# Spectral mixing plus MLP on one core: VectorE and ScalarE work of block 1 behind additions and copies

## The chip, the cores and the metric

The kernel runs on one core of a Trainium2 chip. The metric is the device time of one execution in microseconds, as the median of several runs. The core's engines work side by side, each through its own instructions in a fixed order: TensorE (PE in the profile) multiplies matrices, VectorE (DVE) and ScalarE (ACT) work element by element, GpSimd (POOL) starts some transfers and reduces over partitions, and SyncE (SP) issues most transfers. They wait for each other by semaphores.

## The reference

Tokens `x` (2048 x 576) are normalized; the result is the sum of `x`, a two-dimensional Fourier mixing of the normalized tokens (real part), and a ReLU MLP of them with 4608 hidden units.

```python
def _A_ref(x, dft_seq_re, dft_seq_im, dft_hid_re, dft_hid_im):
    a = jnp.einsum("bsd,ed->bse", x, dft_hid_re)
    b = jnp.einsum("bsd,ed->bse", x, dft_hid_im)
    return jnp.einsum("ts,bse->bte", dft_seq_re, a) - jnp.einsum("ts,bse->bte", dft_seq_im, b)

def _B_ref(x, w1, w2):
    h = jnp.maximum(jnp.einsum("bsd,df->bsf", x, w1), 0)
    return jnp.einsum("bsf,fd->bsd", h, w2)

xn = _layernorm(x, axis=-1)
return x + _A_ref(xn, A_dft_seq_re, ...) + _B_ref(xn, B_w1, B_w2)
```

## The kernel before, in words

Every operand of float32 is split into two float16 halves, a high one (a ScalarE copy) and a low one (a VectorE subtraction), and a product is three float16 matmuls. The weights are scaled by powers of two before they are split: VectorE takes the maximum of their magnitudes (`max_w1`, the reductions at L117 and L625), GpSimd reduces it over the partitions (`power`, L123), VectorE works out the scale from that (L126 to L131: `half`, `c_sw`, `c_pw`), and then `split` (L185 on ScalarE, L186 on VectorE) writes the halves.

The MLP is done in 9 blocks `b` of 512 hidden units by 4 groups `g` of 512 tokens: 36 steps `n`, numbered `b * 4 + g`. One step does the first layer of (b, g) (`mlp1_step`, L346 and L371; four accumulators `p1_b_g_0` to `_3` in PSUM) and, between its parts, the second layer of the step before (`mlp2`, L589), whose seven products 0 to 6 are those of a scheme that needs seven products instead of eight for a 2 x 2 blocked multiplication. This is why sums of blocks are needed: sums of w2's blocks (`sums_w2`, L712 to L715), sums of h's blocks, and, from block 2 on, where the first layer is done by the same scheme, sums of w1's blocks and of the tokens' blocks.

`mlp1_out` takes the hidden values out of PSUM, one pair of accumulators at a time (pair 0 and pair 1 of each step): ReLU to the high halves on ScalarE (L390, L394), the low halves on VectorE (L395), four sums of blocks on VectorE (L399 to L402), their high halves on ScalarE (L404) and their low halves on VectorE (L406). Product 1 of `mlp2` reads what L394 and L395 wrote, products 2 to 5 read the sums.

`mlp2` accumulates products in PSUM places: 0, 2, 4 and 6 in one, 1 in another, 3 and 5 in a third, with two buffers for them all. Behind each product its place is read: by a ScalarE copy (L600) behind products 0, 2, 3 and 6, by a VectorE addition (L603) behind 1, 4 and 5. A product in the same place waits for that reader. So product 6 waits for the addition behind product 4, product 4 for the copy behind product 2, product 5 for the copy behind product 3. GpSimd then adds the sums to HBM (L606, `spill`).

`sums_x` is a generator of 10 pieces a group. Each group needs four sums of token blocks, on VectorE (L469 to L473), with high halves on ScalarE (L453) and low halves on VectorE (L458). Block 2 reads them first. In block 1 `next(tq)` takes a piece behind each product of `mlp2`, and some more at the end of a quarter of the step.

`todo` is a list of the preparations of the next block's weights, in order: loads of w1, its maxima and scale, its splits, loads of w2, their maxima and scale, splits, sums, splits. `work()` takes one piece from it. The raw weights come into two buffers (`raw`), so w2's loads (L100, issued by SP) wait until w1's splits have read theirs. In step 2 (block 0, group 2) block 1's list begins:

```python
if n == 2:
    if i > 1:
        todo += prepare_block(1) if i == 2 else []
        for _ in range(1 if i == 2 else 11):
            work()
    continue
```

A scheduler takes the traced instructions and lays down each engine's order when the kernel is built. `tc.issue_after(ins)` puts the instructions of its block behind `ins` on the same engine, without a semaphore. `behind(key)` does it for the last instruction that was noted under a name: `"vfree"` is VectorE's last addition of a product, `"free"` ScalarE's last copy of one.

Of the kernel before, what the change touches and what calls it, by code (L numbers as in the profile page):

```python
# [13 lines left out]
AF = mybir.ActivationFunctionType  # L14
ALU = mybir.AluOpType
# [34 lines left out]
def kernel(  # L50
# [17 lines left out]
    nc = tc.nc  # L68
# [123 lines left out]
    means, factors, shifts, order = {}, {}, {}, {}  # L192
# [4 lines left out]
    def behind(key):  # L197

        return tc.issue_after(order[key]) if key in order else nullcontext()
# [118 lines left out]
    A11, A12, A22, S1, S2, S3, S4 = range(7)  # L318
# [57 lines left out]
            ps.append(new_ps1(b, g, 0))  # L376
        mlp1_group(b, g, i, slice(0, G), ps[i], WK[:-1], start=(i == 0), stop=(i > 0))

    def mlp1_out(b, g, i, pa, pb, after=None, last=None):

        h = hs[b, g, i] = mlp.tile([P, 2, 7, GH], F16, tag="h", name=f"h{b}_{g}_{i}", bufs=4)
        st = mlp.tile([P, 5, GH], F32, tag="stage", name=f"s{b}_{g}_{i}")
        stt = nc.vector.scalar_tensor_tensor
        a11, a21, a12, a22 = pa[:, :GH], pa[:, GH:], pb[:, :GH], pb[:, GH:]
        r21, s1, s2, s3, s4 = (st[:, n] for n in range(5))
        with behind(after):
            nc.scalar.activation(r21, a21, AF.Relu)  # L390
        for q, src in ((slice(A11, A11 + 1), a11), (slice(A12, A22 + 1), pb)):
            hi, lo = (h[:, n, q].rearrange("p a b -> p (a b)") for n in range(2))
            with behind(after):
                order["hi"] = nc.scalar.activation(hi, src, AF.Relu).ins  # L394
                stt(lo, src, 0.0, hi, ALU.max, ALU.subtract)  # L395

        def sums():
            with behind(last or after):
                stt(s3, a11, 0.0, r21, ALU.max, ALU.subtract)  # L399
                stt(s1, a22, 0.0, r21, ALU.max, ALU.add)  # L400
                stt(s2, a22, 0.0, s3, ALU.max, ALU.subtract)
                stt(s4, a12, 0.0, s2, ALU.max, ALU.subtract)  # L402
            hi, lo = (h[:, n, S1 : S4 + 1] for n in range(2))
            order["s"] = nc.scalar.activation(hi, st[:, 1:], AF.Copy).ins  # L404
            with behind(last):
                order["lo"] = nc.vector.tensor_tensor(lo, st[:, 1:], hi, ALU.subtract).ins  # L406

        if last:
            return sums
        sums()  # L410

# [14 lines left out]
    def halves(g, q):  # L428

        r, c = q  # L430
        k, t = 2 * r, (H1, H2)[c]
        return xT[g][:, k : k + 2, t], xT[g][:, KM + 1 + k : KM + 3 + k, t]
# [7 lines left out]
    def sums_x(g):  # L440

        f = [
            w[:, 2 * KT * P :][:, : 2 * GH].rearrange("p (k t) -> p k t", t=GH) for w in w1bufs[2:]
        ]
        tt = nc.vector.tensor_tensor

        def high(q):
            with tc.issue_after(gates[g][0]):
                nc.scalar.activation(xsums[g][:, q, 0], f[q % 2], AF.Copy)  # L453

        def low(q):
            hi, lo = (xsums[g][:, q, n] for n in range(2))
            with tc.issue_after(gates[g][1]):
                tt(lo, f[q % 2], hi, ALU.subtract)  # L458

        for q, (head, tail) in enumerate((  # L460
            ((0, 1), (0, 0)), ((1, 1), None), ((1, 0), None), ((1, 1), (0, 1)),
        )):
            if q > 1:
                low(q - 2)
            t = f[q % 2]
            h, l = halves(g, head)
            if tail:
                h2, l2 = halves(g, tail)
                tt(t, h, h2, ALU.subtract)  # L469
                tt(t, t, l2, ALU.subtract)  # L470
            else:
                tt(t, h, f[1 - q % 2], ALU.subtract)
            tt(t, t, l, ALU.add)  # L473
            yield
            if q:
                high(q - 1)
            yield
        low(2)
        high(3)
        yield  # L480
        low(3)
        yield

    banks1, ends, gates = [], [], {}
# [534 lines left out]
    for n in range(2, len(steps)):  # L1019
# [46 lines left out]
        ps = []  # L1066
        for i in range(NF):
# [12 lines left out]
                transposes_dma(t, nc.scalar)  # L1080
            if i % 2:
                after = ("w2hi", "vfree")[i // 2] if n == 2 else None
                mlp1_out(b, g, i // 2, *ps[i - 1 : i + 1], after=after)
            if i == (3 if n == 2 else 1):

                gates[n - 2] = order["s"], order["lo"]
            if n == 2:
                if i > 1:
                    todo += prepare_block(1) if i == 2 else []
                    for _ in range(1 if i == 2 else 11):  # L1090
                        work()
                continue
            if b:
                work()
            for q in range(2 * i, min(2 * i + 2, 7)):
                mlp2(pb, pg, q)
                if b:
                    next(tq, None)
                else:
                    for _ in range(2):  # L1100
                        work()
            for _ in range((0, 1, 0, 2)[i] if b else 0):
                next(tq, None)
            for _ in range(1 + i % 2 if b else (2, 2, 2, 4)[i]):
                work()
            if (n, i) > (6, 1) and i % 2 and passes:
# [1 line left out]
        if n == 2:  # L1108
            for q in range(2, 7):
                mlp2(pb, pg, q)  # L1110
    while todo:
        work()
    for q in range(7):
# [239 lines left out]
```

## Time and profile before

| what | value |
|---|---|
| median of 3 runs | 1249.34 us (1249.05 to 1249.57) |
| the profiled execution | 1249.3 us |
| its span in the trace | 1247.5 us |
| mean granted TensorE clock | 0.999 |
| first products of block 2 (L512) in the trace | 200.87 us |

The times of the trace are counted from the span's start. A row of a timeline has the start and the duration in us, the engine, the line, the operation, what it writes and reads, the shape and a count; in brackets stands how long the engine was idle before it, and who released it. The duration of one row runs on into the next by some 0.08 us, so a step is best read from start to start. A row of the waits has the total in us, how often, and the longest. A row of the windows has, for a stretch, the busy time of each engine with its number of instructions, and at its end the granted clock of TensorE (1.00 is full), the share of time in which the transfer engines worked, and GB/s.

### The profile page before, as it was taken

What the parts mean: (1) busy time and instruction counts of PE and PEld (TensorE: products, weight loads), DVE (VectorE), ACT (ScalarE), POOL (GpSimd) and SP (SyncE); (2) the same over time, 40 slices, a digit from 0 to 9 for tenths busy, and PEclk for the clock granted to TensorE, in tenths of its full rate; (3) what the DMA queues carried; (4) which work ended last, traced back from release to release, by engine and by line L of the source; (5) the groups of instructions that cost most, each with busy time, mean ns of one, the idle gap of its engine ahead of it and who ended that gap; (6) DMA issues with size and microseconds to landing.
All of it is one profiled execution on the core that took longest, in us unless ns stands there. A gap on an engine that the chain in (4) does not pass through costs nothing.

```text
span 1247.5 us, 25273 instructions
## 1 busy us (share of the span) xinstructions
PE 1228.4 (98%) x10269; PEld 981.0 (79%) x10269; DVE 1009.1 (81%) x1919; ACT 704.7 (56%) x1192; POOL 158.9 (13%) x207
## 2 busy tenths in 40 slices
PE   8989999999999999999999999999999999999998
PEld 7656557888888888888888888877777777777776
DVE  9999997878878788788787878467787878888885
ACT  5655465676676765766777766545543333333332
POOL 2321221212121211111111112200000000000000
PEclk9999999999999999999999999999999999999999
DMA  9985356757667665666585766620053434443420
GB/s 313 204 134 125 59 85 140 130 126 145 144 103 174 120 150 117 134 139 134 119 176 120 160 128 124 130 83 1 1 173 124 133 117 148 134 127 125 136 87 20
DMA packets 80324, 157.28 MB, mean 126 GB/s; under 512 B 22224, under 2 KB 41168, under 8 KB 80208
## 3 DMA queue, kind: packets, MB, share of 16 engines
q1 hardware_dynamic: 57424, 113.20, 28.6%
q0 software_dynamic: 22784, 42.48, 25.9%
q8 instruction: 80, 1.31, 0.5%
q14 instruction: 36, 0.29, 0.1%
HBM read 104.53 MB, written 51.90 MB: 125 GB/s over the span
## 4 chain that ended last, share of the span: by engine, by line
PE 83%; DVE 7%; ACT 1%; issue 1%; DMA 1%; POOL 0%; POOLq 0%; DVEq 0%; ACTq 0%
PE p L1285 26%; PE p L589 24%; PE bank L512 23%; PE pd L1156 8%; DMA raw_w<-in_w_dram 1%; PE p L346 1%; DVE w2s L186 1%; DVE h L395 1%; DVE dbuf L473 1%; DVE acc L458 0%; DVE c_mf L117 0%; PE pd L1166 0%; DVE w1buf L186 0%; ACT f L1008 0%; DVE dbuf L470 0%
## 5 line engine op out<-in xcount | busy, mean ns | idle before, releaser
L589 PE MATMUL p<-w2s,h 128*128 128x288 f16 x3024 | 410.2, 287 | 9.2 <-DVE c_sw L127 4.1
L589 PEld LDWEIGHTS <-h 128*128 128x128 f16 x3024 | 296.1, 98 | 86.0 <-issue 10.6
L1285 PE MATMUL p<-R,cs 128*128 128x288 f16 x2688 | 329.4, 286 | 0.0
L1285 PEld LDWEIGHTS <-cs 128*128 128x128 f16 x2688 | 263.0, 98 | 66.3
L185 ACT ACTIVATE cs<-c,sc_c 128x1024 f16<-128x1024 f32 x112 | 125.2, 1144 | 196.7 <-DVE c L1218 72.6
L186 DVE SCALAR_TENSOR_TENSOR cs<-c,sc_c,cs 128x1024 f16<-128x1024 f32 x112 | 141.0, 1282 | 54.4 <-ACT cs L185 54.4
L512 PEld LDWEIGHTS <-w1buf 128*128 128x128 f16 x1600 | 156.5, 98 | 21.6 <-issue 0.5
L512 PEld LDWEIGHTS <-dbuf 128*128 128x128 f16 x1200 | 117.4, 98 | 15.8
L512 PE MATMUL bank<-xT,w1buf 128*128 128x256 f16 x832 | 109.8, 273 | 0.0
L1156 PE MATMUL pd<-dbuf,xT 128*128 128x288 f16 x832 | 103.8, 286 | 0.0
L512 PE MATMUL bank<-acc,w1buf 128*128 128x256 f16 x768 | 102.3, 273 | 0.3 <-ACT acc L538 0.3
L534 DVE TENSOR_TENSOR h<-s,h 128x1024 f16<-128x1024 f32 x56 | 68.5, 1224 | 37.9 <-ACT h L531 37.9
L1156 PEld LDWEIGHTS <-xT 128*128 128x128 f16 x832 | 80.8, 98 | 22.0 <-issue 1.9
L606 POOL DMA_DIRECT2D spill<-dbuf x70 | 61.0, 874 | 241.7 <-DVE dbuf L603 214.6
L519 ACT ACTIVATE h<-acc 128x256 f16<-128x256 f32 x112 | 46.0, 411 | 71.5 <-DVE acc L542 70.6
L512 PE MATMUL bank<-xT,dbuf 128*128 128x256 f16 x624 | 82.3, 273 | 0.0
L531 ACT ACTIVATE h<-s 128x1024 f16<-128x1024 f32 x56 | 59.2, 1056 | 35.4 <-DVE s L526 35.1
L512 PE MATMUL bank<-acc,dbuf 128*128 128x256 f16 x576 | 76.6, 273 | 0.0
L1291 DVE SCALAR_TENSOR_TENSOR o<-p,us_c,o 128x288 f32<-128x288 f32 x112 | 57.5, 514 | 12.9 <-PE p L1285 12.5
L600 ACT ACTIVATE dbuf<-p,c_ub 128x576 f32<-128x576 f32 x70 | 51.3, 733 | 22.3 <-PE p L589 22.0
L1008 ACT ACTIVATE f<-f 128x1024 f32<-128x1024 f32 x60 | 62.7, 1046 | 0.4 <-DMA f<-in_cre_dram 0.4
L520 DVE SCALAR_TENSOR_TENSOR h<-acc,h 128x256 f16<-128x256 f32 x112 | 47.3, 422 | 18.7 <-ACT h L519 18.3
(163 smaller groups left out, 1519.8 us busy)
## 6 DMA issues: line engine op xcount, KB each, us to landing
spill<-dbuf POOLq DMA_DIRECT2D x70, 288.0 KB, 5.2
c<-in_cre_dram SPq DMA_DIRECT2D x32, 512.0 KB, 4.3
c<-in_cim_dram SPq DMA_DIRECT2D x32, 512.0 KB, 5.0
f<-in_cre_dram SPq DMA_DIRECT2D x30, 512.0 KB, 5.9
f<-in_cim_dram SPq DMA_DIRECT2D x30, 512.0 KB, 5.8
spill<-sum POOLq DMA_DIRECT2D x42, 288.0 KB, 4.5
raw_w<-in_w_dram SPq DMA_DIRECT2D x17, 640.0 KB, 5.6
raw_w<-in_w_dram SPq DMA_DIRECT2D x18, 576.0 KB, 5.0
```

The lines of the kernel that those rows point to most:

```text
L185: nc.scalar.activation(hi, src, AF.Copy, scale=s).ins,
L186: nc.vector.scalar_tensor_tensor(lo, src, s, hi, ALU.mult, ALU.subtract).ins,
L512: nc.tensor.matmul(ps, l, r, start=first and m == 0, stop=m == len(todo) - 1, skip_group_check=not first,)
L531: order["s"] = nc.scalar.activation(hi_s, st[:, 1:], AF.Copy).ins
L534: order["lo"] = nc.vector.tensor_tensor(lo_s, st[:, 1:], hi_s, ALU.subtract).ins
L589: order["pe"] = nc.tensor.matmul(ps[:, c], h[:, x, qa, c * P : (c + 1) * P], w[:, y, qb], start=first and i == 0 and j == 0, stop=i == NQ ...
L600: freed(nc.scalar.activation(o, ps, AF.Copy, scale=us[b]))
L606: nc.gpsimd.dma_start(spill[g, row, col], o, accum_op=ALU.add)
L1008: nc.scalar.activation(f, f, AF.Abs, scale=2.0**-10, accum_out=sums_c[:, n, q : q + 1])
L1156: nc.tensor.matmul(ps[j], xT[g][:, kx, c * P : (c + 1) * P], dsp[j][:, hl, k], start=(t % 2 == 0 and n == 0), stop=(t % 2 == 1 and n == le ...
L1285: nc.tensor.matmul(ps, w[:, a, k], r[:, c, rq], start=first and k == 0 and j == 0, stop=k == HK - 1 and j == 2, skip_group_check=not first,)
L1291: order["o"] = nc.vector.scalar_tensor_tensor(o, ps, us["c"][:, n : n + 1], o, ALU.mult, ALU.add).ins
```

## The change

Four things are moved; no operation is added or removed.

1. In step 2, 4 pieces of block 1's list are taken at the place where 11 were, and the other 7 behind the last products of `mlp2` of that step. The reductions of the second half of w1 and all of w1's splits therefore stand behind the additions of group 1, and the splits behind those of group 2's first products as the scheduler lays them.
2. For pair 0 in block 1, the high halves of the sums (ScalarE) are emitted behind product 3 and put behind its copy, and the low halves (VectorE) behind product 5 and its addition.
3. The pieces of `sums_x` are taken in three bunches a step, behind products 0, 2 and 3, and 6, instead of one behind each product and some between.
4. For groups 1 to 3 the sums of tokens and their low halves are put behind the last addition of a product.

```diff
-    def mlp1_out(b, g, i, pa, pb, after=None, last=None):
+    def mlp1_out(b, g, i, pa, pb, after=None, last=None, late=False):
...
-        def sums():
+        def values():
             with behind(last or after):
                 stt(s3, a11, 0.0, r21, ALU.max, ALU.subtract)
                 stt(s1, a22, 0.0, r21, ALU.max, ALU.add)
                 stt(s2, a22, 0.0, s3, ALU.max, ALU.subtract)
                 stt(s4, a12, 0.0, s2, ALU.max, ALU.subtract)
-            hi, lo = (h[:, n, S1 : S4 + 1] for n in range(2))
-            order["s"] = nc.scalar.activation(hi, st[:, 1:], AF.Copy).ins
-            with behind(last):
+
+        hi, lo = (h[:, n, S1 : S4 + 1] for n in range(2))
+
+        def high():
+            with behind("free" if late else None):
+                order["s"] = nc.scalar.activation(hi, st[:, 1:], AF.Copy).ins
+
+        def low():
+            with behind("vfree" if late else last):
                 order["lo"] = nc.vector.tensor_tensor(lo, st[:, 1:], hi, ALU.subtract).ins
 
         if last:
-            return sums
-        sums()
+            return lambda: (values(), high(), low())
+        values()
+        if late:
+            return high, low
+        high()
+        low()
...
         def low(q):
             hi, lo = (xsums[g][:, q, n] for n in range(2))
-            with tc.issue_after(gates[g][1]):
+            with tc.issue_after(gates[g][1]), behind("vfree" if g else None):
                 tt(lo, f[q % 2], hi, ALU.subtract)
...
-            if tail:
-                h2, l2 = halves(g, tail)
-                tt(t, h, h2, ALU.subtract)
-                tt(t, t, l2, ALU.subtract)
-            else:
-                tt(t, h, f[1 - q % 2], ALU.subtract)
-            tt(t, t, l, ALU.add)
+            with behind("vfree" if g else None):
+                if tail:
+                    h2, l2 = halves(g, tail)
+                    tt(t, h, h2, ALU.subtract)
+                    tt(t, t, l2, ALU.subtract)
+                else:
+                    tt(t, h, f[1 - q % 2], ALU.subtract)
+                tt(t, t, l, ALU.add)
...
-                mlp1_out(b, g, i // 2, *ps[i - 1 : i + 1], after=after)
+                late = mlp1_out(
+                    b, g, i // 2, *ps[i - 1 : i + 1], after=after, late=bool(b) and i == 1
+                )
...
-                    for _ in range(1 if i == 2 else 11):
+                    for _ in range(1 if i == 2 else 4):
                         work()
...
             for q in range(2 * i, min(2 * i + 2, 7)):
                 mlp2(pb, pg, q)
                 if b:
-                    next(tq, None)
+                    if q in (3, 5):
+                        late[q == 5]()
+                    for _ in range((2, 0, 3, 2, 0, 0, 3)[q]):
+                        next(tq, None)
                 else:
                     for _ in range(2):
                         work()
-            for _ in range((0, 1, 0, 2)[i] if b else 0):
-                next(tq, None)
...
         if n == 2:
             for q in range(2, 7):
                 mlp2(pb, pg, q)
+            for _ in range(7):
+                work()
```

## The prediction

> **What bounds the kernel now.** I read the page first, then the waits of TensorE in stretches, then the windows and the timelines of the engines around each wait, and at last the order in which the changed kernel is built, engine by engine.
>
> ```profile
> span 1247.5 us, 25273 instructions
> ...
> PE 1228.4 (98%) x10269; PEld 981.0 (79%) x10269; DVE 1009.1 (81%) x1919; ACT 704.7 (56%) x1192; POOL 158.9 (13%) x207
> ```
>
> TensorE (PE) is busy in 98% of the span, so only its gaps can be won, and a gap that is added anywhere is paid in full. The change moves nothing on any engine before 78.1 us, and nothing after the first products of block 2 (some 206 us), so the question is what TensorE loses between. Its waits there, first from 60 to 90 us, then from 90 to 215 us:
>
> ```profile
> PE p L589 <- DVE c_sw L127: 4.1, 1, 4.1
> ...
> PE p L589 <- ACT dbuf L600: 1.4, 1, 1.4
> PE p L589 <- DVE acc L603: 1.0, 1, 1.0
> PE p L589 <- DVE sum L603: 0.5, 1, 0.5
> PE bank L512 <- ACT acc L538: 0.3, 1, 0.3
> ```
>
> They make 7.3 us. The clock adds to the first of them (busy time by engine, then the granted clock as PEclk; the third line is the sum over the twelve slices of 10 us from 80 to 200 us):
>
> ```profile
> 79.40:83.50 4.10, 0.01 (x1) 0.00 (x0) 4.10 (x10) 0.98 (x1) 0.38 (x1) 1.00 0.99 120
> 83.50:87.00 3.50, 3.50 (x14) 2.08 (x14) 3.50 (x9) 1.97 (x3) 3.13 (x3) 0.51 0.46 51
> ...
> sum 120.00, PE 113.68 PEld 67.90 DVE 113.07 ACT 65.74 POOL 24.91; mean PE 9.47 PEld 5.66 DVE 9.42 ACT 5.48 POOL 2.08
> ```
>
> After the wait the clock is 0.51 for 3.5 us, which costs 3.5 x 0.49 = 1.7 us. So TensorE loses 7.3 + 1.7 = 9.0 us here: that is all the change can take. The sum line is the second thing to see: VectorE (DVE) is busy for 113.07 of 120 us. It is nearly the bound itself, and the change takes no instruction from it, it only orders them anew.
>
> **Part 1: the addition comes sooner.** VectorE and TensorE around the first wait:
>
> ```profile
> 79.21 1.53 DVE L117 TENSOR_REDUCE c_mf<-raw_w 128x1 f32<-128x640 f32 x2
> 80.66 1.22 DVE L406 TENSOR_TENSOR h<-s,h 128x1024 f16<-128x1024 f32 x1
> ...
> 81.86 0.81 DVE L117 TENSOR_REDUCE c_mf<-raw_w 128x1 f32<-128x640 f32 x1
> ...
> 82.64 0.81 DVE L603 SCALAR_TENSOR_TENSOR acc<-p,c_ub,acc 128x576 f32<-128x576 f32 x1
> ...
> 83.50 3.04 PE L589 MATMUL p<-w2s,h 128*128 128x288 f16 x12 [4.10 <-DVE c_sw L127]
> 86.33 3.26 PE L346 MATMUL p<-xT,w1buf 128*128 128x512 f16 x13
> ```
>
> The page names a tiny c_sw as releaser; what the product 6 of group 1 waits for is the addition at 82.64, which reads the same PSUM place. (A row's duration overlaps the next start by 0.08 us, so I take steps from start to start: the addition 0.73, a reduction 0.73, the subtraction L406 1.13.) In the built order the addition follows the second reduction, which ends at 79.21 + 0.73 = 79.93. Past it go the two reductions of the second half, the subtraction and two tiny ones: 82.64 - 79.93 = 2.7 us. The matmul follows at 83.50 - 2.7 = 80.8, and the wait is 1.4 instead of 4.1. In the slice from 140 to 150 us the 1.4 us wait of the list left the clock whole (the 1.00 ahead of the last two numbers):
>
> ```profile
> 140.00:150.00 10.00, 8.65 (x56) 5.36 (x55) 10.00 (x21) 4.94 (x9) 0.88 (x1) 1.00 0.45 101
> ```
>
> So the 1.7 us of clock go too. Next late are the transposes of the tokens of group 3, which the matmuls at 86.33 read (from their line's answer, the last issued at 77.3):
>
> ```profile
> L284 SPq DMA_TRANSPOSE xT<-dbuf x4: 1350/1781/2721, 71.8 to 77.3; - x4
> ...
> DMA to landing us min/median/max: 3.5/6.0/6.8
> ```
>
> They land at 77.3 + 3.5 to 6.8, or 80.8 to 84.1, with the median at 83.3. A product of 12 matmuls takes 1.47 us (3.10 less 0.16 of overlap for 24 of them in the row of 111.59 below, 0.122 each), so product 6 runs from 80.8 to 82.3, and a new wait of 0 to 1.8 us stands there; I take the median's, 0.9. TensorE begins group 3 at 83.2, and has won 86.33 - 83.2 = 3.1 us, and 0.3 more that the slow clock still cost before behind 86.33.
>
> **Part 2: the weights come later.** The reductions and splits of w1 wait behind group 2's additions now, and everything of w2 hangs on them: its loads go into the raw buffers that the splits free.
>
> ```profile
> 84.87 1.68 DVE L186 SCALAR_TENSOR_TENSOR dbuf<-raw_w,c_sw,dbuf 128x640 f16<-128x640 f32 x2
> 88.58 1.67 DVE L186 SCALAR_TENSOR_TENSOR dbuf<-raw_w,c_sw,dbuf 128x640 f16<-128x640 f32 x2
> ...
> 86.58 4.03 SPq L100 DMA_DIRECT2D raw_w<-in_w_dram  x2
> ...
> 96.28 1.16 ACT L680 ACTIVATE j<-raw_w 128x1152 f32<-128x1152 f32 x1 [1.07 <-DMA raw_w<-in_w_dram]
> ...
> 98.11 0.17 DVE L126 TENSOR_SCALAR half<-top 128x2 f32<-128x2 f32 x1 [0.93 <-POOL top L123]
> 103.72 0.22 DVE L703 TENSOR_SCALAR c_sw<-c_pw,c_inv 128x2 f32<-128x2 f32 x1
> 111.59 3.10 PE L589 MATMUL p<-w2s,h 128*128 128x288 f16 x24
> 111.93 0.69 DVE L395 SCALAR_TENSOR_TENSOR h<-p,h 128x512 f16<-128x512 f32 x1
> ...
> L458 DVE TENSOR_TENSOR acc<-dbuf,acc 128x512 f16<-128x512 f32 x16 | 10.9, 684 | 0.0
> ```
>
> From the end of the addition at 80.66 to the end of the first two splits the built order has on VectorE: the subtraction 1.13, two additions 1.45, two reductions 1.45, eight sums of tokens at 0.60 (L458's group, 684 ns less the overlap) 4.8, two reads of 256 at 0.33, five tiny ones 0.3 and the splits 1.6, together 11.4, and some 0.6 us where one sum waits for the one before: 92.7, against 86.46 in the trace. Up to the other two splits come 3.3 us more (sum, reads of 0.60 and 0.33, splits, tiny ones): 96.0 against 90.17. SP issued the second load at 90.28, it landed at 96.28, and the scale stood on VectorE at 98.11. All of it moves by 5.8: the scale stands at 103.9. Up to c_sw L703, 5.6 us in the trace, the new order has 2.4 us of work (an addition, a sum, two reads, tiny ones): 106.4. The split of w2 follows ScalarE's, 1.2 us later; then two splits at 1.03, all eight w2 sums at 0.37 and one split of 0.73 stand ahead of the read L395 of the last 512 columns of group 3's h: 106.4 + 1.2 + 2.06 + 2.94 + 0.73 = 113.3, and this read is done at 114.0. Before it was done at 112.5.
>
> TensorE needs it at the fourth matmul of product 1: 111.59 + 15 x 0.122 = 113.4 before, so nobody waited. Now it comes 3.4 us earlier, at 110.0, with some 0.2 for ScalarE's copy of product 0, and waits 3.7 us (2.5 to 4.5, by how soon the second load lands). At 114 us TensorE stands 0.5 us later than before: this wait, which the trace of before doesn't have, takes the whole gain of part 1 back.
>
> POOL's maximum of w2 waits for the same load, and group 2's spills queue behind it; no engine waits for them at that time, so they cost nothing. SP issues in the old order.
>
> **Part 3: sums of tokens and high halves behind additions and copies.** These three waits of the list go:
>
> ```profile
> 129.75 0.81 DVE L603 SCALAR_TENSOR_TENSOR acc<-p,c_ub,acc 128x576 f32<-128x576 f32 x1
> 176.38 0.81 DVE L603 SCALAR_TENSOR_TENSOR sum<-p,c_ub,sum 128x576 f32<-128x576 f32 x1
> 148.27 1.06 ACT L404 ACTIVATE h<-s 128x1024 f16<-128x1024 f32 x1 [2.44 <-DVE s L402]
> 149.23 0.72 ACT L600 ACTIVATE dbuf<-p,c_ub 128x576 f32<-128x576 f32 x1
> ```
>
> The addition at 129.75 and the one at 176.38 stood behind sums of tokens, which the new order puts behind them; the copy at 149.23 stood behind the high halves L404, which now follow the copy. That is 1.0 + 0.5 + 1.4 = 2.9 us. But VectorE has its work still to do, and the sums that it did early in block 1 stand late now: 11 of them, 6.6 us, fall into block 1's last step, where the trace of before has none.
>
> ```profile
> 173.81 2.97 PE L346 MATMUL p<-xT,dbuf 128*128 128x512 f16 x13
> 179.94 0.68 DVE L395 SCALAR_TENSOR_TENSOR h<-p,h 128x512 f16<-128x512 f32 x1
> 187.91 3.10 PE L589 MATMUL p<-w2s,h 128*128 128x288 f16 x24
> 189.00 0.68 DVE L395 SCALAR_TENSOR_TENSOR h<-p,h 128x512 f16<-128x512 f32 x1
> 199.40 1.63 PE L589 MATMUL p<-w2s,h 128*128 128x288 f16 x12
> 205.03 0.36 ACT L538 ACTIVATE acc<-bank 128x256 f32<-128x256 f32 x1
> ```
>
> Between the matmuls that end at 187.91 and the product 6 at 199.40 TensorE has 11.5 us of its own. In the new order VectorE needs 9.4 us in this stretch up to the addition that product 6 waits for: reads of h 1.6 and one sum 0.6, then seven sums 4.2, four of w2 1.5, a split 0.73 and the addition 0.73. So it may lag behind TensorE by 2.1 us at no cost. At the half step before, the trace shows a lag of 3.3: the read at 179.94 is of matmuls that end at 173.81 + 13 x 0.216 = 176.6. With 9.9 us of work and 1.2 us of waiting for ScalarE's split against TensorE's 11.3 it stays at about 3.3 to 3.6, so the wait is 1.2 to 1.5; I take 1.5, with 0 (no lag) and 2.5 as ends. The lag also delays the last h of block 1 and the copy L538 behind it on ScalarE, which TensorE waited 0.3 us for: about 1.2 now, from 0.3 to 2.
>
> **The sum.** Lost before 4.1 + 1.7 + 1.0 + 1.4 + 0.5 + 0.3 = 9.0. Lost after 1.4 + 0.9 + 0.2 + 3.7 + 1.5 + 1.2 = 8.9. The profiled execution took 1249.3 us, 1247.5 of span and 1.8 around it, and the median is 1249.34, so the profile stands for it. I forecast 1249.3 - 9.0 + 8.9 = 1249.2, in effect no change; 0.2%, about what a measurement of this kernel tells from none, is 2.5 us.
>
> **The rivals.**
>
> *The clock falls at the new wait (0.2).* The wait of 4.1 us was followed by 1.7 us of slow clock, that of 1.4 us was not; the new one of 3.7 us is nearer to the first. TensorE would be 1.7 us later behind 114 us, and the sums pinned behind its additions would move with it, so nothing takes it up again: 1250.9. Against it speaks that it is the shorter wait. [...]
>
> *VectorE's lag is gone before the last step (0.12).* If the forced wait at 114 us lets it catch up for good, the waits of 1.5 and 1.2 fall away, which decides at a lag under 2.1 us at 188 us: 1249.2 - 2.7 = 1246.5, faster. For it speaks the lag's fall to 1.1 (189.00 - 187.91) in the old order there; against it the 6.6 us of sums which that order did not have in this step.
>
> *VectorE's lag grows (0.1), slower.* Its idle time is 120 - 113.07 = 6.9 us over the twelve slices, and the new order makes it idle where it waits for w2: it has nothing to put between the late load and the scale, some 4 us by the row of 96.28 moved to 102.1. If the remaining 3 us are not enough, each of the last two waits grows by about 1.3: 1249.2 + 2.6 = 1251.8. It decides at a lag of over 5 us at 188 us.
>
> That the change doesn't do what it says is not a rival: the built order shows each move.
>
> **How the numbers follow.** The forecast has 0.58; with its unsure waits (0.9, 3.7, 1.5, 1.2) it lies between 1247.8 and 1250.6. The range takes in the clock's case and the near halves of the two lag cases: 1247.0 to 1251.8. Faster by over 2.5 us, below 1246.8, needs the second rival whole: 0.08. Slower, above 1251.8, needs half of the third, or the clock's case at its upper end: 0.11. Within: 0.81.
>
> **What would show it.** Right: in the waits of TensorE 4.1 is gone, about 1.4 and 0.9 stand near 80 and 83 us, one of 3 to 4.5 us stands near 110 to 114 us with a read of h on VectorE as releaser, the three of 130, 150 and 177 us are gone, and two of 1 to 2 us stand at 197 to 206 us; SP issues w2's loads at about 92.9 and 96.1. Wrong: no wait over 2 us near 112 us, or waits on VectorE in block 2.

## The result, and the profile after

The changed kernel takes 1253.45 us (median of 7 runs, 1252.31 to 1255.61) against 1250.12 us of the kernel before (7 runs): a ratio of 1.0030, 95% interval 1.0019 to 1.0042, so slower by 3.3 us. On a second occasion it took 1254.59 us against 1250.01 (1.0032, 1.0019 to 1.0045). The forecast was 1249.2 in a range from 1247.0 to 1251.8. The profiled execution took 1253.36 us.

The page's head, and the sum line of the windows over the twelve slices of 10 us from 80 to 200 us:

```profile
span 1251.6 us, 25269 instructions
...
PE 1229.7 (98%) x10269; PEld 981.4 (78%) x10269; DVE 1008.1 (81%) x1919; ACT 704.7 (56%) x1192; POOL 159.2 (13%) x207
...
sum 120.00, PE 113.04 PEld 66.58 DVE 106.35 ACT 64.44 POOL 23.49; mean PE 9.42 PEld 5.55 DVE 8.86 ACT 5.37 POOL 1.96
```

The work of every engine over the whole span is nearly the same (PE 1228.4 before, 1229.7 now); VectorE does 6.7 us less of it in these 120 us (113.07 before), because it stands idle more often there. TensorE's waits after, from 60 to 120 and from 120 to 215 us:

```profile
PE p L601 <- DVE h L396: 3.4, 1, 3.4
PE p L601 <- DVE acc L615: 3.2, 2, 1.8
PE p L346 <- issue: 0.7, 1, 0.7
...
PE p L601 <- DVE dbuf L615: 1.8, 1, 1.8
PE bank L524 <- ACT acc L550: 1.1, 1, 1.1
PE p L601 <- ACT dbuf L612: 0.2, 1, 0.2
```

The line numbers are higher than before, by 1 (L395, now L396) to 12 (L589, now L601); L346 and less are unmoved. The forecast's waits are all there: 1.4 and 0.7 in place of 4.1, 3.4 for a read of h, 1.8 and 1.1 at the end; those of 130, 150 and 177 us are gone. One is there that the forecast did not have, the second of the two on `acc`. The timelines of TensorE, VectorE, ScalarE, SyncE's queue and GpSimd around them:

```profile
80.98 1.63 PE L601 MATMUL p<-w2s,h 128*128 128x288 f16 x12 [1.38 <-DVE acc L615]
83.27 2.97 PE L346 MATMUL p<-xT,w1buf 128*128 128x512 f16 x13 [0.66 <-issue]
105.90 1.63 PE L601 MATMUL p<-w2s,h 128*128 128x288 f16 x12 [1.78 <-DVE acc L615]
116.13 1.35 PE L601 MATMUL p<-w2s,h 128*128 128x288 f16 x7 [3.36 <-DVE h L396]
...
103.29 1.22 DVE L413 TENSOR_TENSOR h<-s,h 128x1024 f16<-128x1024 f32 x1 [4.22 <-ACT h L409]
105.03 0.81 DVE L615 SCALAR_TENSOR_TENSOR acc<-p,c_ub,acc 128x576 f32<-128x576 f32 x1
...
101.05 1.16 ACT L692 ACTIVATE j<-raw_w 128x1152 f32<-128x1152 f32 x1 [4.19 <-DMA raw_w<-in_w_dram]
102.21 1.04 ACT L409 ACTIVATE h<-s 128x1024 f16<-128x1024 f32 x1
...
93.32 3.63 SPq L100 DMA_DIRECT2D raw_w<-in_w_dram  x2
...
81.22 1.08 POOL L618 DMA_DIRECT2D spill<-acc  x1 [6.45 <-DVE acc L615]
89.36 0.38 POOL L123 PARTITION_ALL_REDUCE top<-c_mw  x1 [7.06 <-DVE dbuf L484]
```

Read it backwards from 105.90. Product 6 waits for the addition at 105.03, which stands behind L413 at 103.29 in VectorE's order. L413 needs the high half L409, and ScalarE stood still for 4.19 us because its queue has the first sum over w2 (L692) ahead of L409, and that sum's load, issued at 93.32, had only landed at 101.0, 7.7 us later. GpSimd's reduction at 89.36, which w1's splits and so w2's load hang on, came 7.06 us after the spill ahead of it; e4, e8 and e12 are about that. Behind the last wait the clock falls: here are two windows of 3.41 us, cut at the times at which the granted clock changes (TensorE's busy time stands first, the clock third from the end):

```profile
113.29:116.70 3.41, 0.57 (x5) 0.47 (x6) 3.41 (x9) 3.38 (x7) 0.00 (x0) 1.00 0.75 87
116.70:120.12 3.42, 3.42 (x11) 0.80 (x10) 3.42 (x6) 1.38 (x3) 0.00 (x0) 0.50 0.44 148
```

Where the time went shows best when the start of the same matmul is compared between two traces (both have 10269 in almost the same order). The table has the start less that in the trace before, in us, at matmuls that began at the time on the left in it. The first row is the chance of each execution's start, so differences down a column count:

| before | changed | e1 | e2 | e3 | e4 | e5 | e7 | e12 |
|---|---|---|---|---|---|---|---|---|
| 78.0 | +0.19 | +0.24 | +0.08 | +0.33 | +0.47 | -0.21 | +0.67 | -0.35 |
| 90.0 | -3.36 | -3.23 | +1.29 | -3.24 | -2.83 | -3.70 | -2.89 | -3.76 |
| 108.0 | -1.42 | -0.88 | +1.29 | -3.24 | -2.83 | -3.40 | -2.89 | -3.77 |
| 120.1 | +4.17 | +4.78 | +1.29 | +2.44 | -1.62 | -2.13 | -1.48 | -2.85 |
| 178.1 | +0.72 | +1.32 | -2.17 | -1.02 | -5.08 | -5.58 | -3.39 | -6.31 |
| 1240 | +3.73 | +1.51 | +0.84 | +2.19 | -1.96 | -3.17 | -1.45 | -2.95 |

For the changed kernel the steps are -3.55, +1.94, +5.59, -3.45 and +3.01, together +3.5. The forecast's terms in the same places: -(4.1 + 1.7) + 1.4 + 0.9 = -3.5; 0; 0.2 + 3.7 = +3.9; -2.9; 1.5 + 1.2 - 0.3 = +2.4; together -0.1. Two steps carry the miss: 1.9 us at 106, and 1.7 us between 108 and 120, where the clock falls.

### The profile page after: what moved, and what is told of

Read it like the earlier page. It is cut to its first block, busy times and chain, and to the rows that moved or that the text cites. A ratio compares the mean times of both kernels' runs of the same rounds, so it can differ in the third digit from the quotient of the medians.

```text
span 1251.6 us, 25269 instructions
## 1 busy us (share of the span) xinstructions
PE 1229.7 (98%) x10269; PEld 981.4 (78%) x10269; DVE 1008.1 (81%) x1919; ACT 704.7 (56%) x1192; POOL 159.2 (13%) x207
## 4 chain that ended last, share of the span: by engine, by line
PE 83%; DVE 8%; ACT 1%; issue 1%; DMA 1%; POOL 0%; DVEq 0%; POOLq 0%; ACTq 0%
PE p L1302 26%; PE p L601 24%; PE bank L524 23%; PE pd L1173 8%; PE p L346 1%; DVE h L413 1%; DVE w2s L186 1%; DVE h L396 1%; DMA raw_w<-in_w_dram 1%; DVE dbuf L485 1%; DVE w1buf L186 0%; PE pd L1183 0%; DVE acc L469 0%; DVE dbuf L615 0%; ACT w2s L185 0%
## 5 line engine op out<-in xcount | busy, mean ns | idle before, releaser
L601 PE MATMUL p<-w2s,h 128*128 128x288 f16 x3024 | 409.2, 286 | 10.7 <-DVE acc L615 3.7
L601 PEld LDWEIGHTS <-h 128*128 128x128 f16 x3024 | 295.5, 98 | 87.0 <-issue 8.5
```

The costliest lines, as they stand in the source:

```text
L601: order["pe"] = nc.tensor.matmul(ps[:, c], h[:, x, qa, c * P : (c + 1) * P], w[:, y, qb], start=first and i == 0 and j == 0, stop=i == NQ ...
```

## The experiments

The letters of the theories are set anew in each expectation. The leading theory throughout is this: the deferral (item 1 of the change) makes w2's load and scale late; this costs the wait at 106, the one at 116 and the slow clock, and the sums and high halves (items 2 to 4) take and give the same. Rivals: the late sums cost; the load or GpSimd's reduction is slow whatever the order; the clock's loss is given back.

**e1, the deferral alone, and e2, the sums alone.** The kernel before with 4 + 7 pieces of the list; the changed kernel with 11 pieces and none behind:

```diff
# e1, from the kernel before
-                    for _ in range(1 if i == 2 else 11):
+                    for _ in range(1 if i == 2 else 4):
...
+            for _ in range(7):
+                work()
...
# e2, from the changed kernel
-                    for _ in range(1 if i == 2 else 4):
+                    for _ in range(1 if i == 2 else 11):
...
-            for _ in range(7):
-                work()
```

> The kernel before with the deferral alone (4 steps of block 1's preparation ahead of group 1's remaining products, 7 behind them); the sums and high halves stay where they were. Theory A (the deferral makes w2 late, and this is what the change costs): TensorE's wait of 4.1 us at 79 becomes about 1.4 + 0.7, and new waits of about 1.8 us near 106 and 3.4 us near 116 stand there as in the changed kernel, while the waits of 1.0, 1.4 and 0.5 us at 130, 150 and 177 shrink, because VectorE has had time: 1250 to 1253 us, slower than before by 0 to 3 us. Theory B (the sums and high halves, late in block 1, are what costs): no new waits over 1 us between 100 and 120, and 1246 us or less.

> The changed kernel without the deferral (11 steps ahead of group 1's remaining products, as before): only the sums and high halves move. Theory A: the wait of 4.1 us at 79 and the slow clock behind it stay, nothing new near 106 and 116, the waits at 130, 150 and 177 (2.9 us) go, and those of VectorE's lag at 197 to 209 stand at 0.3 to 2.9 us: 1247 to 1249.5 us, faster than before by 0.8 to 3 us. Theory B: waits of 3 us and more on VectorE in block 1's last two steps, 1251 us or more.

Measured: e1 1250.81 us (ratio 1.0006, 0.9997 to 1.0014), e2 1249.96 us (1.0001, 0.9992 to 1.0009); e2 lies 0.5 us above its theory A's range. Neither is clear of noise against the kernel before. TensorE's waits in their timelines, e1 and then e2:

```profile
106.43 1.63 PE L589 MATMUL p<-w2s,h 128*128 128x288 f16 x12 [2.19 <-DVE acc L603]
...
117.28 1.03 PE L589 MATMUL p<-w2s,h 128*128 128x288 f16 x7 [2.96 <-DVE h L395]
```

```profile
83.58 3.04 PE L601 MATMUL p<-w2s,h 128*128 128x288 f16 x12 [4.10 <-DVE c_sw L127]
...
199.47 1.63 PE L601 MATMUL p<-w2s,h 128*128 128x288 f16 x12 [1.75 <-DVE dbuf L615]
206.27 0.81 PE L524 MATMUL bank<-acc,w1buf 128*128 128x256 f16 x6 [1.06 <-ACT acc L550]
```

e1 has the two new waits with no late sum in it, as theory A has it, and its median is 0.8 us above the kernel before; e2's is level with it (its +1.29 at 90 us comes with a granted clock of 0.50 for 6.83 us, 82.60 to 89.43, behind the old wait of 4.1 us in this execution, where the kernel before has it for 3.41). Yet both together lose 3.3. The table says why: from 120 to 178 us e1 wins 3.46 us (4.78 to 1.32) though its sums stand in the old places, e2 wins the same 3.46, and the changed kernel 3.45. The waits of 130, 150 and 177 us go either because the sums stand behind, or because TensorE has been held up until VectorE caught up (e7, which does neither, has some of them again). Done twice, it is won once, while the price of the late sums, 3.0 us from 178 on, is paid in full (3.01 us in e2 and in the changed kernel, 0.19 in e1).

**e3, ScalarE's sum behind the copy.** From the changed kernel; the built order moves this one instruction.

```diff
-        with behind("free" if b >= BB else None if b else after):
+        with behind("free" if b >= BB else ("s" if i == 0 else None) if b else after):
             nc.scalar.activation(
                 junk, raws["w2", b, i], ...
```

> The changed kernel with one edit: ScalarE's first sum over w2 stands behind the copy of the high half of h of group 3 instead of ahead of it. Theory A (the load of w2 holds that copy through ScalarE's queue, and through it VectorE's subtraction and the addition behind it): VectorE's idle time of 4.2 us ahead of the subtraction moves behind the addition, the wait of 1.8 us at 106 is gone, the wait of 3.4 us for h at 116 shrinks by the 2 us of work that VectorE has done meanwhile, and the total is 1.8 to 4.5 us below the changed kernel (1249 to 1251.6 us). Theory C (the addition is late for another reason, or TensorE loses the same time at 116): the total stays within 1 us of the changed kernel, with a wait of 4 to 5 us at 116.

Measured: 1252.69 us (1.0021, 1.0012 to 1.0031). ScalarE, VectorE and TensorE:

```profile
98.01 1.06 ACT L409 ACTIVATE h<-s 128x1024 f16<-128x1024 f32 x1 [1.04 <-DVE s L403]
100.37 1.16 ACT L692 ACTIVATE j<-raw_w 128x1152 f32<-128x1152 f32 x1 [1.30 <-DMA raw_w<-in_w_dram]
...
103.96 0.17 DVE L126 TENSOR_SCALAR half<-top 128x2 f32<-128x2 f32 x1 [2.31 <-POOL top L123]
...
113.60 0.68 DVE L396 SCALAR_TENSOR_TENSOR h<-p,h 128x512 f16<-128x512 f32 x1
...
114.34 1.03 PE L601 MATMUL p<-w2s,h 128*128 128x288 f16 x7 [3.35 <-DVE h L396]
```

The wait at 106 is gone, as theory A has it: ScalarE's queue was its cause. The wait for h comes 1.8 us sooner and is as long as before, where theory A had it 2 us shorter: VectorE's work done ahead only became idle time in front of the scale (2.31 us at 103.96), because what L396 stands behind still hangs on the load. In the table e3 stands 1.7 us better than the changed kernel at 1240 us, each counted from 78 us. The medians are less sure: 1252.69 lies above theory A's range, 0.8 us below the changed kernel's first median of 1253.45 and 1.9 below its second of 1254.59, and the intervals of the ratios overlap. The wait and its cause are shown; what the time gains is not clear of noise.

**e6, a filled wait.** From the changed kernel; 40 matmuls of 128 columns of zeros into columns of the accumulator that nobody reads, ahead of the matmul that waits.

```diff
...
+                    if (b, g, n, c, i, j) == (0, 3, 1, 0, 1, 2):
+                        for _ in range(40):
+                            nc.tensor.matmul(
+                                full[n][:, 0, EH : EH + P], idle[:, :P], idle[:, :P],
+                                start=True, stop=True, skip_group_check=True,
+                            )
```

> The changed kernel with 40 matmuls of 128 columns of zeros, into columns that nobody reads, ahead of the matmul of group 3's product 1 that waits 3.4 us for h; they take some 2.7 to 3.3 us and end before h is there. Theory A (the slow clock follows from TensorE being idle, and its 1.7 us are paid in full): the granted clock is 1.00 from 105 to 125 us, TensorE stands where it stood at 116 and 1.7 us sooner at 122, and the total is 1251 to 1252.3 us, 1.2 to 2.4 below the changed kernel. Theory B (VectorE, which follows TensorE, gives the time back later, or the slow clock has another cause): within 0.7 us of the changed kernel's 1253.4.

Measured: 1252.30 us (1.0016, 1.0007 to 1.0025), 1.15 below the changed kernel's first median. The windows and TensorE's rows:

```profile
113.29:116.70 3.41, 1.97 (x27) 1.51 (x24) 3.41 (x9) 2.84 (x5) 0.00 (x0) 1.00 0.70 85
116.70:120.12 3.42, 3.27 (x17) 1.21 (x16) 3.42 (x6) 1.60 (x3) 0.00 (x0) 1.00 0.55 183
```

```profile
111.97 2.40 PE L605 MATMUL p<-idle 128*128 128x128 f16 x40
115.81 1.03 PE L609 MATMUL p<-w2s,h 128*128 128x288 f16 x7 [1.44 <-DVE h L396]
```

The matmul that waits comes when it came before, with nothing won but the clock, which stays at 1.00. Theory A holds, at the upper end of its range: with TensorE busy for 1.97 of the 3.41 us from 113.29, in place of 0.57, the fall is gone. The slow stretch of 3.42 us at half the clock counts for 1.7 us; with the same matmuls compared as in the table and the filler left out, e6 is 1.2 us ahead of the changed kernel from 120 us to the end, counted from 78 us. By the medians it is 1.15 us, or 2.3 by the second one.

**e9, both edits of e3 and e6.**

> The changed kernel with both single edits: ScalarE's first sum over w2 behind the copy, and 40 matmuls of zeros ahead of the one that waits for h. Theory A (the wait of 1.8 us at 106 and the slow clock are separate losses, each paid in full): 1249.8 to 1250.9 us, 1.4 to 2.4 below the kernel with the filler alone (1252.3). Theory B (half of the wait at 106 is given back behind it, as the 0.8 us of the experiment with the copy first suggest): 1251.1 to 1252.0 us.

Measured: 1251.46 us (1.0013, 1.0004 to 1.0022), by its median in theory B's range, but the runs lie between 1248.79 and 1253.70, which covers both. The profiled execution was the slowest; in it GpSimd's first reduction came at 91.18 and not at 89.36, and TensorE waited 2.28 us for a copy (L620) ahead of the filler, with a granted clock of 0.50 behind it from 112.14 to 115.56. So this run doesn't decide between them.

**e4, GpSimd's reduction first.** From the changed kernel; one spill of group 1 behind the first reduction of w1's maxima. In the built order GpSimd's reduction precedes that spill again, as in the kernel before, and the scheduler, with the same deferral, lays the first splits of w1 ahead of group 2's first addition.

```diff
-        nc.gpsimd.partition_all_reduce(top, m, P, ReduceOp.max)
+        order["ar"] = nc.gpsimd.partition_all_reduce(top, m, P, ReduceOp.max).ins
...
+            with behind("ar" if (b, g, n) == (0, 1, 4) else None):
                 nc.gpsimd.dma_start(spill[g, row, col], o, accum_op=ALU.add)
```

> The changed kernel with one edit: GpSimd issues the spill of group 1's first added quarter behind the first reduction of w1's maxima, not ahead of it. The planner then also builds the splits of w1 earlier (the first two behind the second reduction of the second half, the other two behind group 2's first addition), and the addition that TensorE waits for stays where the changed kernel has it. Theory A (late splits of w1 make w2 late): the reduction runs near 82 instead of 89.4, w2's first load is issued near 88 instead of 93.3, the waits at 106 and 116 are gone, 2 us stay near 80 to 83, and the late waits of VectorE stand at 2 to 5 us: 1245.5 to 1249 us. Theory D (the load is slow by itself, or the reduction runs late wherever it is issued): the reduction still ends 7 us after the spill before it or the load still takes over 7 us, and a wait of over 1.5 us stays between 100 and 120: 1250 us or more.

Measured: 1247.77 us (0.9982, 0.9973 to 0.9991), faster than both. GpSimd, SyncE's queue and TensorE:

```profile
73.97 1.08 POOL L619 DMA_DIRECT2D spill<-acc  x1 [6.41 <-DVE acc L615]
82.54 0.38 POOL L123 PARTITION_ALL_REDUCE top<-c_mw  x1 [7.49 <-DVE c_mw L638]
...
86.98 5.94 SPq L100 DMA_DIRECT2D raw_w<-in_w_dram  x2
...
81.26 1.63 PE L601 MATMUL p<-w2s,h 128*128 128x288 f16 x12 [1.39 <-DVE acc L615]
111.52 1.03 PE L601 MATMUL p<-w2s,h 128*128 128x288 f16 x7 [0.52 <-DVE h L396]
```

The early addition and the early load go together: w2's load is issued 6.3 us sooner than in the changed kernel, no wait stands at 106, 0.5 is left of the 3.4, and the granted clock is 1.00 from 100 to 120 us. The medians of e4 and the changed kernel are 5.7 us apart.

**e7, the same without the sums.** The kernel of e1 with e4's two edits.

> The kernel before with the deferral alone and the reduction ahead of the spill, so the experiment with the reduction first without the later sums and high halves. Theory A (the sums and high halves give and take the same): the waits of 1.4 and 0.9 us at 80 to 84 stand there, those of VectorE at 130 to 177 come back at 2 to 4 us because TensorE is ahead again, none stand at 190 to 204 but the 0.3, and the total is within 1 us of 1247.8. Theory B (they gain once TensorE is no longer held up at 116): over 1249 us. Theory C (they cost): under 1246.5 us.

Measured: 1247.33 us (0.9976, 0.9966 to 0.9986): theory A by the total. The waits that come back are smaller than its 2 to 4 us, and half of them are on ScalarE's copies: four from 150 to 193 us, together 1.6, and 0.6 instead of 0.3 ahead of block 2's bank. The table's columns have what the sums and high halves give and take: from 120 to 178 us e7 wins 1.9 and e4 3.5, from there on e7 loses 1.9 and e4 3.1.

**e5, the sums sooner**, from e4: five of the 40 pieces of `sums_x` are taken in block 1's first step, where VectorE stands idle for 4.1 of the 13 us from 120 to 133 us in e4.

```diff
-                    for _ in range((2, 0, 3, 2, 0, 0, 3)[q]):
+                    for _ in range(((2, 0, 3, 2, 0, 0, 3), (2, 2, 3, 2, 1, 2, 3))[n == 4][q]):
```

> The kernel of the experiment with the reduction first, and five of the 40 steps of sums of tokens taken sooner: in block 1's first step the counts behind the seven products are 2, 2, 3, 2, 1, 2, 3 instead of 2, 0, 3, 2, 0, 0, 3, so the sums of group 3 end half a step sooner. Theory A (the waits of 1.8, 1.1 and 0.2 us at 190 to 204, which stood alike in every kernel with the late sums, are made by the seven sums that stand ahead of the addition in block 1's last step, while VectorE stands idle for some 5 us between 120 and 133): they go and nothing takes their place, 1244.5 to 1245.8 us. Theory B (VectorE's work as a whole is the bound, so the lag only moves): waits on VectorE of 2 us or more together stand between 130 and 190 instead, 1246.5 to 1248.5 us.

Measured: 1247.57 us (0.9977, 0.9967 to 0.9986). No wait is left between 120 and 200 us, but one of 2.7 has taken the place of 1.75 + 1.06 + 0.17 (VectorE and TensorE):

```profile
195.16 1.22 DVE L413 TENSOR_TENSOR h<-s,h 128x1024 f16<-128x1024 f32 x1
196.29 0.81 DVE L186 SCALAR_TENSOR_TENSOR w2s<-raw_w,c_sw,w2s 128x576 f16<-128x576 f32 x1
...
197.36 0.68 DVE L396 SCALAR_TENSOR_TENSOR h<-p,h 128x512 f16<-128x512 f32 x1
...
202.28 0.82 PE L524 MATMUL bank<-acc,w1buf 128*128 128x256 f16 x6 [2.71 <-ACT acc L550]
```

The total lies in theory B's range, but its waits between 130 and 190 us are not there, so neither theory holds: the sums are out of the way, and now the last h of block 1 (L396, whose matmuls had ended at 194.0) stands behind a subtraction and a split of w2 on VectorE, with the copy L550 behind it on ScalarE.

**e11, the count sooner**, from e5: ScalarE's sums over the transform's matrix, one half step sooner.

```diff
-            if (n, i) > (6, 1) and i % 2 and passes:
+            if (6, 0) < (n, i) < (7, 3) and i % 2 and passes:
```

> The kernel with the reduction first and the sums sooner, with one edit more: of the three sums of the DFT's first pass in block 1 each is taken one half step sooner, so that none stands on ScalarE ahead of the copy of the bank in block 2's first product. Theory A (TensorE's wait of 2.7 us at 202 is that sum of 1.1 us, and the lag of VectorE's last h for the rest): the wait is 1.5 to 1.7 us, 1246 to 1246.8 us. Theory B (the sum only fills time in which ScalarE would wait anyhow): 1247.2 to 1248 us, with a wait of 2.4 us or more.

Measured: 1246.10 us (0.9971, 0.9960 to 0.9982), the fastest kernel here, 3.9 us below the kernel before. Its wait is 2.55 us, not 1.5 to 1.7, as theory B had it, so theory A has the time and not the reason. The interval also holds e5's ratio, and in the traces the two are level: at 1240 us e5 is 2.96 and e11 2.99 us ahead of the kernel before, counted from 78 us. That this edit gains anything is not shown.

**e8 and e12, the first reduction ahead of time.** Both add one reduction, of a column that nobody uses, to the changed kernel and leave the spill ahead of w1's reduction: in e8 behind group 0's first added quarter, in e12 right behind GpSimd's last work on tokens. The scheduler then lays VectorE's order as in e4.

```diff
# e8
                 nc.gpsimd.dma_start(spill[g, row, col], o, accum_op=ALU.add)
+            if (b, g, n) == (0, 0, 4):
+                with behind("acc"):
+                    nc.gpsimd.partition_all_reduce(cell("ld", 1), accs[0][:, 3, EH : EH + 1], P, ReduceOp.max)
...
# e12
     sums_s = mlp1_out(0, 1, 1, *q2, after="w2", last="vfree")
+    ld = cell("ld", 2)
+    nc.scalar.activation(ld[:, :1], hs[0, 1, 0][:, 0, 0, :1], AF.Copy)
+    nc.gpsimd.partition_all_reduce(ld[:, 1:], ld[:, :1], P, ReduceOp.max)
```

> The changed kernel with one more reduction on GpSimd, of a column that nobody uses, behind group 0's first added quarter, so that the first one of w1's maxima is not the first of its kind; the spill stays ahead of it. Theory A (the 7.1 to 7.5 us between the spill and the first reduction in every trace so far are paid once, by the first reduction of the program, and the planner, which counts them too, puts the splits of w1 late because of them): the reduction of w1's maxima runs near 82.3, the splits of w1 stand as in the experiment with the reduction first, w2's first load is issued near 88, no wait over 1 us stands between 84 and 120, and the total is 1247 to 1248.7 us. Theory B (it is the spill ahead of the reduction that delays it): the reduction still runs near 89, and a wait of over 1.5 us stands between 100 and 120, 1250 us or more.

> The changed kernel with an extra reduction of one unused column on GpSimd right behind its last work on tokens, near 45 us, where it stands idle for 15 us; ScalarE makes the column by one small copy. The spill of group 1 stays ahead of the reduction of w1's maxima; the built order of TensorE, VectorE and SyncE is that of the kernel with the reduction first. Theory A (the first reduction of a program costs some 7 us, and in the changed kernel these stand behind the spill instead of behind the one before, which is why w1's splits come late): the reduction of w1's maxima runs near 82.5, no wait of over 1 us between 85 and 120, the transposes come as in the changed kernel (a wait of 0.6 to 1.0 at 83), and the total is 1247 to 1248.5 us, as with the reduction first. Theory B (the spill issued ahead of the transposes' end or of w2's load also costs): 1249 us or more, with a load of over 7 us or a wait of 2 us or more at 83.

Measured: e8 1254.82 us (1.0042, 1.0028 to 1.0056), e12 1247.24 us (0.9981, 0.9972 to 0.9990). GpSimd, SyncE's queue and TensorE of e8, then GpSimd of e12, and last GpSimd of the kernel before:

```profile
71.55 1.68 POOL L621 PARTITION_ALL_REDUCE c_ld<-acc  x1 [6.88 <-issue]
73.11 3.53 POOL L618 DMA_DIRECT2D spill<-acc  x3
...
82.55 0.42 POOL L123 PARTITION_ALL_REDUCE top<-c_mw  x1
...
72.31 12.23 SPq L284 DMA_TRANSPOSE xT<-dbuf  x4
...
89.09 5.05 PE L346 MATMUL p<-xT,w1buf 128*128 128x512 f16 x13 [6.17 <-issue]
```

```profile
49.05 0.43 POOL L922 PARTITION_ALL_REDUCE c_ld<-c_ld  x1 [6.03 <-ACT h L395]
...
80.68 1.08 POOL L618 DMA_DIRECT2D spill<-acc  x1 [6.45 <-DVE acc L615]
81.69 0.43 POOL L123 PARTITION_ALL_REDUCE top<-c_mw  x1
```

```profile
82.08 0.38 POOL L123 PARTITION_ALL_REDUCE top<-c_mw  x1 [7.49 <-DVE c_mw L625]
```

In both, w1's reduction follows the spill at once (in e8 that spill starts at 81.54), as theory A has it: the gap of 7.06 us that the changed kernel has there is gone, and 6.88 us (e8) and 6.03 us (e12) stand ahead of the added reduction instead. In the kernel before no such gap stands behind the maxima: GpSimd was idle for 7.49 us, VectorE wrote them until 81.94, and the reduction began at 82.08. That the same cost lies in those 7.49 us is inferred. In the changed kernel they were there at 82.13, but the spill at 81.22 stood ahead, and the reduction began at 89.36.

e12 has the built order of e4 on VectorE, TensorE and SyncE with the spill left where the changed kernel has it, and e4's time. In e8 the 6.88 us held up three spills, which went out from 73.11 on together with the token transposes; SyncE took 12.23 us to issue these (7.92 in the changed kernel), TensorE waited 6.17 us for them, and the 13 matmuls behind that wait took 5.05 us (2.97 in the changed kernel). So e8's total is not theory A's 1247 to 1248.7; it lies in theory B's range, but w1's reduction ran at 82.55 and not near 89, and the long wait is not between 100 and 120. That the spills made the transposes slow is inferred from their coming together; no run separates it.

**e10, the changed kernel again.**

> The changed kernel itself, beside the others on the same chip: 1253 to 1254 us. Its trace has the waits of 1.8 and 3.4 us at 106 and 116 again, and the clock falls behind the second of them again if that does not hang on chance; if it hangs on chance, runs without it stand near 1252.

Measured: 1254.59 us (5 runs, 1253.46 to 1254.65). The waits in its trace are 2.18 at 106 and 3.35 at 117, and the granted clock is 0.50 behind the second, from 116.51 to 119.93. The median is 0.6 us above what was expected, and no run is near 1252.

## Why the prediction was wrong, and where it was right

*Part 1, right:* 1.4 and 0.9 us in place of 4.1, measured 1.38 and 0.66; TensorE won 3.55 us by 90 us, 3.4 forecast.

*Part 2, the first failed step.* Its chain ran from the splits over the load and the scale to h; the rows bear it out (load issued at 93.32, 92.9 forecast; L396 at 115.39, 113.3 forecast, and at 113.60 in e3; a wait of 3.36, 3.7 forecast), except that it is the sixth matmul of product 1 that waits and not the fourth. It asked what queues behind the late load on GpSimd ("no engine waits for them") and on SyncE, and did not ask it of ScalarE. There the sum over w2 stands ahead of a copy that VectorE needs, and behind VectorE's subtraction stands an addition that TensorE needs. The forecast had VectorE idle ahead of the scale, but not what queued behind the idle place. The term that it put at nothing is the wait of 1.78 us at 105.90, 1.9 us in the table. e3 shows it: with the sum behind the copy this wait is gone.

*The clock, the second failed step.* That the clock stays whole behind the new wait was in the sum; that it falls was a rival with a chance of 0.2, and it came: 1.7 us by the slow stretch, 1.2 by e6's trace, 1.15 to 2.3 by its medians. The price was about right and the chance was not. The 0.2 was the author's estimate, and no run shows it: all four traces with waits of 2.96 to 3.36 us for h have the fall, as the last section shows.

*Part 3, right in its sum and wrong in its reason.* 2.9 us were counted for the sums behind the additions. The changed kernel wins 3.45, but e1 wins 3.46 without moving a sum, so that the sum came out is in part luck. The forecast took the waits of 130, 150 and 177 us from a trace in which TensorE is early, and did not ask whether they stand there still once TensorE waits 3.7 us at 114. The late waits were of the right kind and size: 1.75, 1.06 and 0.17 where 1.5 and 1.2 were forecast, the same in e2, e3 and e4, so they depend on nothing that went before.

*Rivals two and three:* VectorE's lag was neither gone nor grown; that the late waits are alike to 0.02 us whether TensorE had waited 5.1 us between 100 and 120 (the changed kernel) or 0.7 (e4) shows that they don't hang on what went before; e5, where the sums end sooner and these waits are gone, shows that the late sums make them.

What the forecast took as given, that the splits come late in the built order, turns out to be the root, together with GpSimd's late reduction: e4 and e12 keep the deferral, have the reduction at 82 us and the splits early, and are 5.7 to 6.2 us faster than the changed kernel's first median. Not separated are the two: whether GpSimd's late reduction would delay VectorE by itself stays open, because the order had been laid by the scheduler for a late one and the reduction's reader stands behind an addition that came at 89.28 anyway.

## What to carry to other kernels

When a change makes a load later, go through every engine's queue for what stands behind the first instruction that needs it, and follow each to TensorE. Waits that two parts of a change both remove are won once, while each part's own costs are paid in full: cost every part on the trace as the other leaves it. And before an instruction that comes late once (here GpSimd's first reduction, 7.06 us after the work ahead of it in the changed kernel) is moved past something, look for the idle place in which this did not show (here the 7.49 us of the kernel before): e12 gets back all that the change lost, and 2.9 us more, with a first reduction where the engine has nothing else to do.

## What the runs showed of the hardware

**The clock.** In the trace of the kernel before the granted clock is 0.50 from 83.50 to 86.91 us, in that of the changed kernel from 17.72 to 21.13 and from 116.70 to 120.12: 3.41 us each time, with 1.00 between 5 and 1247 us otherwise. TensorE was not idle for all of the 3.41 us ahead of every fall. Such a stretch and the next one, of e3 and of e5, and the first such pair of e10:

```profile
112.16:115.57 3.41, 1.23 (x8) 0.69 (x8) 3.41 (x8) 3.04 (x6) 0.00 (x0) 1.00 0.59 80
115.57:118.99 3.42, 3.42 (x9) 0.97 (x9) 3.42 (x6) 1.06 (x1) 0.00 (x0) 0.50 0.66 208
```

```profile
200.36:203.77 3.41, 1.49 (x13) 1.27 (x13) 2.62 (x4) 3.35 (x8) 0.00 (x0) 1.00 0.92 288
203.77:207.18 3.41, 3.41 (x32) 2.86 (x30) 1.79 (x4) 0.84 (x3) 0.86 (x1) 1.00 1.01 303
```

```profile
102.86:106.27 3.41, 1.76 (x9) 0.69 (x7) 2.08 (x3) 3.21 (x8) 0.84 (x1) 1.00 0.07 29
106.27:109.68 3.41, 2.88 (x19) 1.86 (x19) 3.15 (x13) 0.60 (x2) 2.18 (x2) 1.00 0.35 24
```

In e3 TensorE was busy for 1.23 of 3.41 us and 0.50 followed; in e5 it was busy for 1.49 and in e10 for 1.76, and 1.00 followed. Of the other stretches of 3.41 us, those with 0.00 (the kernel before, from 80.08), 0.29 (e2, from 79.19), 0.57 (the changed kernel, from 113.29, and e10, from 113.10), 0.93 (e1, from 114.80) and 1.24 (e9, from 108.73) were followed by 0.50, those with 1.54 (e1, from 104.56) and 1.97 (e6, from 113.29) by 1.00. Two others with more work were also followed by 0.50: 1.88 from 14.30 us in the changed kernel, in a stretch of short matmuls near its start, and 2.43 from 82.60 in e2, at 0.50 already. Why is open.

The four traces with waits of 2.96 to 3.36 us for h (the changed kernel, e1, e3 and e10) all have 0.50 behind it, for which the prediction had a chance of 0.2. None of the 87 timed runs of the kernel before that stand beside the experiments has a mean granted clock of 1.000, while 21 of 39 runs of e4, e5, e11 and e12 do.

**The first reduction.** GpSimd's first partition reduction came 7.06 us after the end of the work ahead of it in the changed kernel (7.18 in e10 and 8.76 in e9, which have its order on GpSimd), 6.88 in e8 and 6.03 in e12. In e12 the profile names a ScalarE write (L395) as what ended the 6.03 us, so how much of them was a wait for the column is not shown. The next one came at once in both: at 82.55 in e8, behind the spill of 1.08 us from 81.54, and at 81.69 in e12, behind the spill of 1.08 us from 80.68. What GpSimd did in these gaps no row shows.
